# Gate and up projections beside no attention: each 512-token matmul as two of 256 tokens

## The chip, the cores and the metric

The kernel runs on one core of a Trainium2 chip. The metric is the device time of one execution in microseconds (us); smaller is better. "Before" is the kernel as it stands, "after" is the kernel with the change below.

## What is computed

One transformer block on one sequence of 2048 tokens of width 576: a pre-normalised attention with 32 heads of width 18 that share one key and one value head, then a pre-normalised gated feed-forward layer with no nonlinearity.

```
h  = x + softmax(q k^T / sqrt(18)) v @ wo        q, k, v from layernorm(x)
g  = layernorm(h) @ w_gate                       576 -> 4608
u  = layernorm(h) @ w_up                         576 -> 4608
h2 = h + (g * u) @ w_down                        4608 -> 576
```

Every matrix product of the projections is made in a high and a low part: an operand is split into `hi` (rounded to the matmul's number format, fp32r) and `lo` (the rest), and three products hi·hi, hi·lo and lo·hi are summed. That is where the number three in the loops below comes from.

## The kernel before

The tokens are worked on in four blocks of 512 (`TB`), numbered `b` = 0 to 3. A first part makes keys, values, queries and the split weights of the down projection. Then the attention of block `b` + 1 runs beside the feed-forward layer of block `b`: while block 0, 1 and the first part of 2 are in the feed-forward layer (`ffn`), there are still attention pieces to be done, and they are woven in between its matmuls. Attention ends inside block 2. From there to the end the feed-forward layer runs alone: 13 of the 36 steps of block 2 and all 36 of block 3, 49 steps in all. The variable `on` is true while attention is left (`self.more(b + 2)`), and false in those 49 steps.

One step `f` of `ffn` makes 128 of the 4608 gate and up columns for the 512 tokens. The 576 input features lie in nine chunks of 64 (`c`), and each chunk has three products (`wk`, `xk`), 27 in all, counted by `j`. Each of the 27 is a pair of matmuls: gate with the weights in partitions 0 to 63 (`o` = 0) and up with the weights in partitions 64 to 127 (`o` = 64). Both have 64 rows, 128 columns of weights and 512 columns of moving data `X`. Weights are `ws`, already split by `split_w` one step ahead; the moving data is the normalised, transposed input of the block. While `on`, the results go to two PSUM tiles `pg` and `pu`; otherwise to the two halves of one tile `gu`, one bank each:

```
for o, ps in ((0, pg), (64, pu)):
    pe.matmul(ps, w[o:o + 64, wk, c], X[o:o + 64, xk, c], start=(j == 0), stop=(j == 26))
```

Every matmul instruction comes with a weight load of its own in TensorE's instruction stream (the row PEld of the profile), which the engine may run beside an earlier matmul. `start` clears the accumulation marks of the bank that it writes.

After the 27 pairs, ScalarE copies gate out of PSUM (`g`, line 853), VectorE multiplies it with up (`hf`, line 857), and every second step the products are split and combined (`left_first`, `left`, `left_sums`) into the stationary operands `A` of the down projection. `down` (lines 739 to 805) takes two steps' worth of columns at a time, as 14 groups of three matmuls with 288 columns into the tile `y` (line 795, 42 matmuls); its results are added to `h` by VectorE (line 798) or by way of a ScalarE copy (line 802) and GpSimd (line 803). In the stage without attention, TensorE's order is therefore: 54 pairs of two steps, then 42 down matmuls of the steps before, and so on. Nothing schedules this but the order of the program, so each engine runs its instructions in the order in which the code issues them, waiting on semaphores.

`split_w` of the next step is issued at `j == 3`, its weights come by DMA into `wr`; `load_wd` fetches the seven pieces of down weights after each `down`.

Of the kernel before, what the change touches and what calls it, by code (L numbers as in the profile page):

```python
# [27 lines left out]
TB = 512  # L28
# [6 lines left out]
HT = TB // 2  # L35
# [23 lines left out]
class Block:  # L59
# [755 lines left out]
    def ffn(self, b):  # L815
        pe, act, dve = self.pe, self.act, self.dve
        X, hid, todo = self.X, [], None
        for f in range(NF):
            n_ = NF * b + f
            k = f % 2  # L820
            w = self.ws.pop(n_)
            on = self.more(b + 2)
            last = f == NF - 1 and b + 1 < NB
            if on:
                pg, pu = self.ps_f(f"pg{n_}"), self.ps_f(f"pu{n_}")
            else:
                gu = self.ps_s(f"gu{n_}")
                pg, pu = gu[:, 0], gu[:, 1]
            j = 0
            for c in range(9):  # L830
                for wk, xk in ((0, 0), (0, 1), (1, 0)):
                    if on and not last and j % 4 == 0 and self.more(b + 2):
                        self.pair()
                    for o, ps in ((0, pg), (64, pu)):
                        pe.matmul(ps, w[o:o + 64, wk, c], X[o:o + 64, xk, c], start=(j == 0), stop=(j == 26))  # L835
                    if j == (8 if on else 2) and todo and not plain(n_ - 2):
                        self.left_sums()
                    if j == 3:
                        self.split_w(n_ + 1)
                    if j == 5 and k:  # L840
                        self.left_first(n_ - 1, hid[0])
                    if j == 12:
                        self.run_aux(within=True)
                    if j == 21 and b == f == 0:
                        self.flush(len(self.pend))
                    if j == 6 and last:
                        self.normal(b + 1)
                    j += 1
            if todo and not on:
                drain(self.down(b, *todo))  # L850
                self.load_wd(self.n_wd + 7)
            g = self.hh.tile([P, TB], F32, tag="g", bufs=1, name=f"g{n_}")
            act.copy(g, pg)  # L853
            if on and not last and self.more(b + 2):
                self.pair()
            hf = self.hh.tile([P, TB], F32, tag="hf", bufs=2, name=f"hf{n_}")
            dve.tensor_tensor(hf, pu, g, ALU.mult)  # L857
            hid.append(hf)
            if k:
                self.left(n_ - 1, hid)  # L860
                hid = []
            self.flush(len(self.pend))
            if todo and on:
                drain(self.down(b, *todo))
                self.load_wd(self.n_wd + 7)
            if f < NF - 1:
                self.run_aux()
            todo = (f // 2,) if k else None
        if b + 1 < NB:
            both(self.spread(b + 1), self.down(b, *todo))  # L870
            self.load_wd(self.n_wd + 4)
            if b + 2 < NB:
                self.load_x(b + 2)
        else:
            drain(self.down(b, *todo))
# [207 lines left out]
def both(a, b):  # L1083

    live = [a, b]
    while live:
        live = [x for x in live if next(x, drain) is not drain]


def plain(n):  # L1090

    return n % NF == NF - 2
# [23 lines left out]
def drain(gen):  # L1116
    for _ in gen:
        pass
# [78 lines left out]
```

## Time and profile before

| | before |
|---|---|
| time, median of 3 runs | 2339.83 us (2338.97 to 2340.36) |
| the profiled execution's own time | 2337.37 us |
| its span, first to last instruction | 2335.6 us |
| TensorE busy (PE) | 2287.6 us, 98% of the span |
| weight loads busy (PEld) | 1601.8 us, 69% |
| VectorE, ScalarE, GpSimd busy | 50%, 61%, 28% |
| mean granted TensorE clock | 0.995 |
| stage without attention | 1858.4 us to the end |

All rows come from one profiled execution. "PE" rows are matmuls, "PEld" rows are the weight loads, which overlap them. The duration of one matmul in a row is from its start to its end, and the next matmul starts long before that end, so the time that one matmul costs is read from the distance between starts: a row of the timeline that merges n matmuls lasts (n - 1) distances and the duration of one. Line numbers are those of the kernel before; in the kernel after, everything behind line 835 stands two lines further down.

### The profile page before, as it was taken

Reading aid. Unit: us, or ns where it says so; the run is one execution under the profiler, and the core shown is the slowest. Engines: PE = TensorE matmul, PEld = TensorE weight load, DVE = VectorE, ACT = ScalarE, POOL = GpSimd, SP = SyncE. Lnnn points to the kernel's source line nnn. Section 1 sums busy time; section 2 is a strip of 40 time slices with the busy share of each in tenths; the row PEclk is TensorE's granted clock in tenths of the full one; section 3 lists DMA queues with packets and bytes.
Section 4 is the critical chain, followed back from the end, with each engine's and each line's share of the span. In section 5 each row is a group of like instructions: output and inputs, shape, how many; then the busy total and the mean of one; then the engine's idle time right before and its main releaser. Section 6 shows DMA issues by size and latency. Waiting matters only on the chain.

```text
span 2335.6 us, 46068 instructions
## 1 busy us (share of the span) xinstructions
PE 2287.6 (98%) x18225; PEld 1601.8 (69%) x18225; DVE 1175.2 (50%) x2064; ACT 1433.0 (61%) x1867; POOL 650.1 (28%) x803
## 2 busy tenths in 40 slices
PE   5999999999999999999999999999999999999999
PEld 4434434676777777767777766767777778888888
DVE  7566644344444445444444445444444476565665
ACT  4788886767676766667676766667676623222322
POOL 3544500122222221222222221312222234333333
PEclk9999999999999999999999999999999999999999
DMA  4588962343334333533433433634333345655453
GB/s 141 192 275 267 311 204 78 94 128 123 118 123 128 123 121 98 183 116 122 127 121 120 123 119 101 186 119 128 123 123 110 115 141 189 197 188 179 168 168 127
DMA packets 157842, 345.16 MB, mean 148 GB/s; under 512 B 16095, under 2 KB 48351, under 8 KB 157623
## 3 DMA queue, kind: packets, MB, share of 16 engines
q1 hardware_dynamic: 155031, 331.56, 44.4%
q0 software_dynamic: 2592, 10.62, 1.5%
q8 instruction: 145, 2.38, 0.4%
q14 instruction: 74, 0.61, 0.1%
HBM read 272.63 MB, written 55.67 MB: 141 GB/s over the span
## 4 chain that ended last, share of the span: by engine, by line
PE 81%; DVE 2%; issue 1%; ACT 1%; DMA 1%; POOL 0%; SPq 0%; DVEq 0%; ACTq 0%; POOLq 0%
PE y L795 17%; PE pg L835 15%; PE acc L511 15%; PE gu L835 12%; PE pu L835 10%; PE s L506 9%; PE yo L634 3%; PE y L753 1%; ACT P L507 1%; PE ye L753 0%; PE tx L683 0%; DMA X<-X 0%; DMA out_dram<-h 0%; DVE h L798 0%; DVE h L635 0%
## 5 line engine op out<-in xcount | busy, mean ns | idle before, releaser
L507 ACT ACTIVATE P<-s 128x1024 f32<-128x1024 f32 x1024 | 1026.3, 1027 | 305.0 <-PE s L506 226.1
L835 PE MATMUL pg<-X,ws 64*128 64x512 f32 x2565 | 699.8, 391 | 0.0
L835 PE MATMUL pu<-X,ws 64*128 64x512 f32 x2565 | 699.8, 391 | 0.0
L803 POOL TENSOR_TENSOR h<-h,tmp 128x288 f32<-128x288 f32 x408 | 318.6, 810 | 878.7 <-ACT tmp L802 877.2
L835 PEld LDWEIGHTS pg<-X,ws 64*128 64x128 f32 x2565 | 477.0, 186 | 59.7 <-DMA wdo<-wd_dram 0.8
L835 PEld LDWEIGHTS pu<-X,ws 64*128 64x128 f32 x2565 | 474.5, 186 | 35.1
L511 PE MATMUL acc<-P,V 128*32 128x512 f32 x4096 | 490.7, 599 | 0.7 <-ACT P L507 0.6
L506 PE MATMUL s<-q,kT 56*128 56x512 f32 x2048 | 437.1, 423 | 5.0 <-ACT P L507 2.3
L795 PEld LDWEIGHTS y<-wdo,room 128*128 128x128 f32 x2856 | 387.7, 189 | 51.9 <-issue 43.3
L795 PE MATMUL y<-wdo,room 128*128 128x288 f32 x2856 | 404.8, 300 | 4.8 <-DVE h L798 4.8
L802 ACT COPY tmp<-y 128x288 f32<-128x288 f32 x408 | 163.0, 400 | 330.4 <-PE y L795 324.8
L798 DVE TENSOR_TENSOR h<-h,y 128x288 f32<-128x288 f32 x544 | 235.7, 453 | 242.8 <-PE y L795 240.1
L506 PEld LDWEIGHTS s<-q,kT 56*128 56x128 f32 x2048 | 194.0, 184 | 208.4 <-ACT P L507 116.3
L835 PE MATMUL gu<-X,ws 64*128 64x512 f32 x2646 | 308.3, 389 | 0.3 <-DMA X<-X 0.2
L93 POOL CAST ws<-wr 128x1152 fp32r<-128x1152 f32 x144 | 168.2, 1168 | 430.9 <-PE pu L835 172.6
L835 PEld LDWEIGHTS gu<-X,ws 64*128 64x128 f32 x2646 | 250.8, 184 | 51.3 <-issue 4.0
L511 PEld LDWEIGHTS acc<-P,V 128*32 128x32 f32 x4096 | 114.4, 109 | 247.7 <-issue 241.9
L94 DVE TENSOR_TENSOR ws<-wr,ws 128x1152 fp32r<-128x1152 f32 x144 | 195.6, 1358 | 79.7 <-POOL ws L93 79.7
L857 DVE TENSOR_TENSOR hf<-pu,g 128x512 f32<-128x512 f32 x95 | 65.7, 692 | 332.2 <-ACT g L853 332.2
L94 DVE TENSOR_TENSOR room<-S,room 128x1024 fp32r<-128x1024 f32 x68 | 83.3, 1225 | 159.0 <-ACT room L93 159.0
L853 ACT COPY g<-gu 128x512 f32<-128x512 f32 x49 | 28.9, 590 | 134.8 <-PE gu L835 134.8
L93 ACT CAST room<-hf 128x256 fp32r<-128x256 f32 (+1 forms) x144 | 73.9, 513 | 49.2 <-DVE hf L857 49.0
(162 smaller groups left out, 1572.0 us busy)
## 6 DMA issues: line engine op xcount, KB each, us to landing
wdo<-wd_dram SPq DMA_DIRECT2D x492, 288.0 KB
wr<-in_wgu_dram SPq DMA_DIRECT2D x144, 576.0 KB
wd_dram<-wd_room SPq DMA_DIRECT2D x20, 1008.0 KB
q<-q_dram SPq DMA_DIRECT2D x64, 216.0 KB
q_dram<-qs SPq DMA_DIRECT2D x16, 504.0 KB
X<-X SPq DMA_DIRECT2D x28, 256.0 KB
wd_dram<-wd_hi SPq DMA_DIRECT2D x7, 1008.0 KB
wd_dram<-wd_src SPq DMA_DIRECT2D x7, 1008.0 KB
```

The source lines that it names most:

```text
L93: (copy or self.cast)(hi, src)
L94: self.dve.tensor_tensor(lo, src, f32(hi), ALU.subtract)
L506: self.pe.matmul(s_[:, i], self.kT[o:o + 56, t * P:(t + 1) * P], q[o:o + 56, pr], start=True, stop=True)
L507: self.act.activation(p_, s_, AF.Exp, scale=SCALE)
L511: self.pe.matmul(acc[32 * j:32 * j + 32, :], self.V[:, t, :], Ps[j // 2][:, j % 2, :], start=(t == 0), stop=(t == NT - 1), skip_group_chec ...
L634: pe.matmul(y[:, :HD], m, k, start=(i == 0), stop=(i == len(ms) - 1))
L795: pe.matmul(y[:, :HD], m[:, t * P:(t + 1) * P], k, start=(first and j == 0), stop=(j == 2), skip_group_check=True)
L798: dve.tensor_tensor(hs, hs, y[:, :HD], ALU.add)
L802: act.copy(z, y[:, :HD])
L803: pool.tensor_tensor(hs, hs, z, ALU.add)
L835: pe.matmul(ps, w[o:o + 64, wk, c], X[o:o + 64, xk, c], start=(j == 0), stop=(j == 26))
L857: dve.tensor_tensor(hf, pu, g, ALU.mult)
```

## The change

In the 49 steps without attention, each pair of 512-column matmuls becomes two pairs of 256 columns: first gate and up for the first 256 tokens, then gate and up for the other 256, with the same weights. While attention is beside them, the loop body is what it was.

```diff
-                    for o, ps in ((0, pg), (64, pu)):
-                        pe.matmul(ps, w[o:o + 64, wk, c], X[o:o + 64, xk, c], start=(j == 0), stop=(j == 26))
+                    for t in range(0, TB, TB if on else HT):
+                        q = slice(t, t + (TB if on else HT))
+                        for o, ps in ((0, pg), (64, pu)):
+                            pe.matmul(ps[:, q], w[o:o + 64, wk, c], X[o:o + 64, xk, c, q], start=(j == t == 0), stop=(j == 26), skip_group_check=not on)
```

`HT` is 256. The mark-clearing `start` stays on the very first matmul of each bank; the second half's first matmul finds the marks of its columns cleared and overwrites. In the instruction order of the kernel after, 54 gate and up matmuls of a step without attention have become 108 of 256 columns; ScalarE, VectorE, GpSimd and the DMA queues have the same instructions and the same waits, in the same order.

## The prediction
> **What bounds the kernel now.** I read the page first: its busy line and its chain. Then the stage that the change touches, by windows, and then single stretches of TensorE's timeline, because the price of a matmul is the distance between two starts.
>
> ```profile
> span 2335.6 us, 46068 instructions
> PE 2287.6 (98%) x18225; PEld 1601.8 (69%) x18225; DVE 1175.2 (50%) x2064; ACT 1433.0 (61%) x1867; POOL 650.1 (28%) x803
> ...
> PE 81%; DVE 2%; issue 1%; ACT 1%; DMA 1%; POOL 0%; SPq 0%; DVEq 0%; ACTq 0%; POOLq 0%
> ```
>
> TensorE is busy for 98% of the span and makes 81% of the chain that ended last. Whatever lengthens its stream lengthens the kernel. The stage without attention, whole and then line 835 alone:
>
> ```profile
> 1858.30:2324.50 466.20, 459.40 (x3723) 397.20 (x3721) 285.00 (x505) 135.78 (x267) 168.96 (x198) 1.00 0.52 172
> ```
> ```profile
> 1858.30:2324.50 466.20, 308.21 (x2646) 250.79 (x2646) 1.00 0.52 172
> ```
>
> The columns are PE, PEld, DVE, ACT and POOL busy, the granted clock, DMA share and GB/s. TensorE works 459.40 of 466.20 us; VectorE has 181 us free, the others more, and DMA is half used. So nothing covers a longer TensorE, and nothing else becomes late before it does. Gate and up have 308.21 us there: 49 steps of 27 pairs, 1323 pairs. Loads are busy 250.79 us in it.
>
> **The price of a pair now.**
>
> ```profile
> 1891.71 6.51 PE L835 MATMUL gu<-X,ws 64*128 64x512 f32 x56
> ```
> ```profile
> L835 PEld LDWEIGHTS gu<-X,ws x2646: 182/184/187, 1858.4 to 2323.9; 64*128 64x128 f32 x189
> L835 PE MATMUL gu<-X,ws x2646: 383/386/501, 1858.4 to 2324.2; 64*128 64x512 f32 x189
> ```
>
> 56 matmuls are 28 pairs: (6.51 - 0.386) / 27 = 226.8 ns from pair to pair, so 113.4 ns is what half a pair may cost for the change to be free. The maximum of 501 ns against a median of 386 is a matmul that had to wait for its own load, at the head of a stretch: one load uncovered costs some 115 ns. That it is 115 and not twice this says that the two loads of a pair (rows 0 to 63 and 64 to 127) run side by side. And since the ordinary matmul takes 386, its load is covered.
>
> **The change part by part.** It adds, per pair, two matmuls and two loads; 2646 of each in all. It moves nothing else: the other engines' order and waits stay, every `j` still comes at the same place, and the last matmul of a step, on which ScalarE's copy waits, is still the last. The columns streamed per pair are the same 512. So the question is what 256 columns cost with a load each time. Three things can set it: the stream, the load, the start.
>
> The load. The row that shows loads alone is the one in which the matmul has nearly no columns:
>
> ```profile
> 55.95 1.44 PE L312 MATMUL psv<-C,kvw 18*128 18x18 f32 x12 [2.66 <-DVE kvw L239]
> ```
> ```profile
> L312 PE MATMUL psv<-C,kvw x16: 261/268/288, 55.9 to 58.5; 18*128 18x18 f32 x16
> ```
>
> (1.44 - 0.268) / 11 = 106.5 ns from one 128-column load to the next, with 18 columns of matmul. This is the floor of half a pair, however fast the stream: 2 x 106.5 = 213.0, 13.8 ns below today's pair, times 1323 is 18 us less. The loads of the stretch of 56 matmuls above, which began at 1891.71, begin here:
>
> ```profile
> 1891.72 0.41 PEld L835 LDWEIGHTS gu<-X,ws 64*128 64x128 f32 x4
> ```
>
> So the next pair's loads start within 0.01 us of this pair's matmuls. 106.5 fits under 113.4, with 7 ns to spare less that start. Today the spare is 120 ns. I take the load as covered, but barely.
>
> The start. The short matmuls of this stage are the down projection's, 288 columns with a load of 128 columns each:
>
> ```profile
> 2149.82 3.54 PE L795 MATMUL y<-wdo,room 128*128 128x288 f32 x25
> ```
> ```profile
> L795 PEld LDWEIGHTS y<-wdo,room x2856: 186/188/330, 436.9 to 2317.8; 128*128 128x128 f32 x191
> L795 PE MATMUL y<-wdo,room x2856: 288/295/442, 436.9 to 2317.9; 128*128 128x288 f32 x191
> L795 PEldq EVENT_SEMAPHORE  x410: 51/51/51, 441.2 to 2316.7; - x137
> ```
>
> (3.54 - 0.295) / 24 = 135.2 ns per matmul. At the rate of the long pair (226.8 / 512 = 0.443 ns per column) 288 columns would be 127.6, so a short matmul costs 7.6 ns more than its columns. Not all of this need come back here: these matmuls have 410 extra semaphore waits on the load side among them, and all 128 rows in one load. The ends for a half are then 113.4 (nothing per start) and 121.0 (all 7.6). I take the middle, 117.2, because the row's 7.6 ns holds waits that gate and up don't have, and because I see no row of short matmuls that costs nothing extra. Per pair 2 x 117.2 - 226.8 = 7.6 ns; times 1323 = **10.1 us**. The ends are 0 and 2 x 7.6 x 1323 = 20.1 us.
>
> The head of each stretch stays. Two steps together show it:
>
> ```profile
> 2153.28 12.54 PE L835 MATMUL gu<-X,ws 64*128 64x512 f32 x108
> ```
>
> 53 x 226.8 + 386 = 12406 ns, so 0.13 us of 12.54 are the head, one uncovered load of the same 128 columns and a few uneven pairs. The load before the first matmul is as long after the change; cost nothing, as nothing about it changes.
>
> Who waits on the longer stretch: ScalarE for the copy out of `gu`, GpSimd for `ws` to come free, VectorE for `g`.
>
> ```profile
> ACT g L853 <- PE gu L835: 134.8, 26, 8.4
> ...
> POOL ws L93 <- PE gu L835: 102.1, 22, 8.0
> DVE hf L857 <- ACT g L853: 84.2, 25, 4.6
> ```
>
> All of them wait for TensorE already, none the other way; they wait longer by what TensorE loses, and nothing else comes late. TensorE itself waits for hardly anything in this stage but this:
>
> ```profile
> PE y L795 <- DVE h L798: 4.8, 2, 3.6
> ```
>
> 3.6 us of it is one stall, for VectorE's additions, and does not hang on line 835's length.
>
> The sum against the profiled execution: 2337.37 + 10.1 = 2347.5 us. Its median neighbours are 2.46 us higher (2339.83), so **2349.9 us** in a median of runs, 0.43% slower.
>
> **A rule against the trace.** The Trainium skill, "TensorE: Matmul & The Clock Gate", Part 3 on packing small matmuls, says that a weight load overlaps a matmul in flight only when it targets another row group. This trace does not agree: the load for rows 0 to 63 has only matmuls of its own row group and of the other half before it, and the 386 against 501 ns show it covered. By the rule each half would show its load, 113.4 + 106.5, a pair 440 ns, and the kernel 282 us longer; the long pairs of today would show it too, so I give it no chance of its own.
>
> **The rivals.**
>
> *Nothing happens.* Load 106.5 under stream 113.4, no cost per start: 2340 us, up to 2344 with a ns or so per matmul. For it: 7 ns of margin, and no wait in the chain that belongs to loads. Against it: the 7.6 ns of the 288-column row. It would also come out so if the second load of the same weights were left out; that it isn't is shown by line 795, where two of each three matmuls have the same stationary operand and there are still 2856 loads for 2856 matmuls. Chance 0.24.
>
> *Faster.* The long pair's 226.8 ns may hold something per matmul that grows with its length, such as a stall late in the stream when the load is long done, and shorter matmuls would shed it. Then the load's pace sets the half. Between the floor of 106.5 and 113.4 it would be about 110, a pair 220, 6.8 ns x 1323 = 9 us less: 2331 us. It decides as soon as half a pair is under 111.6 ns (4.7 us less). Nothing in the rows shows it. Chance 0.07.
>
> *The supply of instructions.* A pair is now four instructions in 226.8 ns, 57 each. The densest long stretch I find is the attention's value matmuls:
>
> ```profile
> 1849.41 3.18 PE L511 MATMUL acc<-P,V 128*32 128x512 f32 x27
> ```
> ```profile
> L511 PE MATMUL acc<-P,V x4096: 592/592/1061, 64.9 to 1852.0; 128*32 128x512 f32 x196
> ```
>
> Groups of four, six distances in 3.18 - 0.592: 431 ns for eight instructions, 54 each. The change asks for eight in 226.8, 28 each, twice what any stretch shows. If the queue can't be fed faster than these rows, a pair takes 431 ns and the kernel (431 - 227) x 1323 = 270 us more, 2610 us. Against it: the value matmuls are themselves bound by their columns (512 each, none of the 3.18 us idle), so 54 is what they ask for and not a limit that they show. The same size of loss would come if two loads of different rows took turns (213 per half, 199 ns per pair, 263 us), which the 501 ns of the head speaks against. Together 0.09.
>
> The same page, Part 2 on issuing a matmul, gives some 62 ns per matmul in the sequencer where the hardware does not decode them: an estimate of 4 x 62 = 248 ns per pair, 28 us more. The rows above have no long stretch with matmuls closer than 106 ns on average, so none can refuse it.
>
> *A middle loss.* Half a pair between 121 and 127 ns, because load and start add up where the spare is 7 ns (106.5 + 7.6 + the few ns by which the load starts late): up to 2 x 13.6 x 1323 = 36 us, 2360 to 2376. Chance 0.14.
>
> **How the numbers follow.** My forecast case, a half between 115.2 and 121 ns, 2344.5 to 2360 us, has 0.46. A measurement of this kernel can tell about 0.2%, 4.7 us, from no change. Faster 0.07; same 0.24; slower 0.46 + 0.14 + 0.09 = 0.69. The range runs from 2337 (the no-change case with its noise) to 2372 (most of the middle loss); outside lie the faster case, the supply case and a little of the middle loss, about 0.2.
>
> **What the profile after would show.** Line 837 with 5292 matmuls and 5292 loads on `gu`, 64x256. Two steps together, 216 matmuls, last 12.54 us now; at my price 12.54 + 54 x 0.0076 = 12.95, less what a shorter last matmul saves. A merged row of n matmuls gives the half pair directly: 113 says that loads and starts are hidden, 117 my forecast, 121 the full start cost, 125 and more that load and start add up, 215 that supply or loads in turn bind. The 42 down matmuls between should keep their 5.9 us. I am wrong if the half pair is outside 115 to 121, or if the time moves in another line than 837.

## The result and the profile after

The kernel after takes 2349.37 us (median of 5 runs, 2348.63 to 2354.76), the kernel before 2338.97 in the same comparison (2337.3 to 2340.36): 1.005 times as long, 95% interval 1.0036 to 1.0065. The forecast was 2349.9. The total is right; the steps behind it are right less often, as the traces show, and part of the agreement is luck.

The page after, its first lines and its chain:

```profile
span 2347.1 us, 51360 instructions
PE 2300.3 (98%) x20871; PEld 1665.0 (71%) x20871; DVE 1169.8 (50%) x2064; ACT 1431.8 (61%) x1867; POOL 645.9 (28%) x803
...
PE 82%; DVE 1%; ACT 1%; issue 1%; POOL 0%; DMA 0%; SPq 0%; DVEq 0%; ACTq 0%; POOLq 0%
```

5292 instructions more, 2646 matmuls and 2646 loads, and TensorE as full as before. The stage without attention now, line 837 alone (PE and PEld busy, with their counts):

```profile
1857.20:2336.00 478.80, 324.10 (x5292) 318.98 (x5292) 1.00 0.51 168
```

Before, loads were busy 250.79 of 308.21 us; now 318.98 of 324.10. That alone doesn't say that loads set the pace. The pace is read from a merged stretch (a row that merges n matmuls of one line), the durations of single matmuls and loads from the group of line 837:

```profile
1891.83 3.40 PE L837 MATMUL gu<-X,ws 64*128 64x256 f32 x54
...
2158.47 13.21 PE L837 MATMUL gu<-X,ws 64*128 64x256 f32 x216
2171.61 5.92 PE L795 MATMUL y<-wdo,room 128*128 128x288 f32 x42
```
```profile
L837 PEld LDWEIGHTS gu<-X,ws x5292: 182/188/190, 1857.2 to 2335.6; 64*128 64x128 f32 x196
L837 PE MATMUL gu<-X,ws x5292: 271/280/385, 1857.2 to 2335.8; 64*128 64x256 f32 x196
```

54 matmuls are 27 half pairs: (3.40 - 0.280) / 26 = 120.0 ns from half to half, where 113.4 was the price of no change. Two steps together last 13.21 us instead of 12.54, and the 42 down matmuls behind them 5.92, as before. So the loss is in line 837.

Where the span's 11.5 us are, summed over the distances between neighbouring matmul starts in both traces:

| between starts of | before, us | after, us | difference |
|---|---|---|---|
| gate and up to gate and up (2621 and 5267 distances) | 298.97 | 317.24 | +18.3 |
| last gate and up matmul to first down matmul (23) | 7.25 | 4.72 | -2.5 |
| the same, to the transposes and to the last block's end (2) | 0.63 | 0.41 | -0.2 |
| within the down matmuls (990) | 143.81 | 140.94 | -2.9 |
| first matmul of the kernel to the first of the stage | 1844.15 | 1842.82 | -1.3 |

The rest of the span, 40.8 us before and 40.9 after, is the other matmuls of the stage and the two ends.

The second row is a real saving of the change: the down matmuls start 205 ns after the start of the last gate and up matmul instead of 315, since that one is 280 ns long instead of 386. 1.2 us of the fourth row come from the change, too: TensorE's two waits for VectorE (`PE y L795 <- DVE h L798`) are 3.6 us together instead of 4.8, the longer one 2.9 instead of 3.6 (total, number, longest; after):

```profile
PE y L795 <- DVE h L798: 3.6, 2, 2.9
```

In the longer one, VectorE is held up by weights of the output projection (`wor`), which SyncE fetches during the stretch of gate and up ahead of these down matmuls and GpSimd casts. The timeline before and then after, transfer, first down matmul and cast:

```profile
1870.51 0.47 SPq L596 DMA_DIRECT2D wor<-in_wo_dram  x1
...
1870.85 1.45 PE L795 MATMUL y<-wdo,room 128*128 128x288 f32 x9
...
1873.40 0.67 POOL L93 CAST wos<-wor 128x576 fp32r<-128x576 f32 x1 [7.38 <-DMA wor<-in_wo_dram]
```
```profile
1869.17 0.47 SPq L596 DMA_DIRECT2D wor<-in_wo_dram  x1
...
1870.34 1.46 PE L795 MATMUL y<-wdo,room 128*128 128x288 f32 x9
...
1872.21 0.67 POOL L93 CAST wos<-wor 128x576 fp32r<-128x576 f32 x1 [7.05 <-DMA wor<-in_wo_dram]
```

The transfer starts 0.34 us ahead of the down matmuls before, 1.17 us after: the longer stretch covers more of it. The runs below bear this out. The two waits together fall as the two steps get longer: 4.8 us at 12.54 (before), 4.3 at 12.82 (narrower weights), 3.6 at 13.21 (after), 3.1 at 13.51 (unequal parts), 0.9 at 14.53 (parts of 288 columns).

The rest of the fourth row, and the fifth, are not the change's. In the profiled execution of before, the clock that TensorE was granted fell to half for 3.4 us twice, here behind the longer wait; in that of after it did not at these places. The same part of the down matmuls (window, matmuls and loads, clock), before and then after:

```profile
1876.70:1880.10 3.40, 3.40 (x16) 3.40 (x15) 0.50 0.32 87
```
```profile
1875.40:1878.80 3.40, 3.39 (x26) 3.16 (x24) 1.00 0.45 104
```

A down matmul takes 240 ns at the clock of 0.50, against a median of 132 at 1.00, and the 15 distances from the first slowed matmul on are 1.5 us longer than the same 15 after. The other such stretch, 1378.3 to 1381.7 us, lies ahead of the stage, in instructions that both kernels share, and costs 1.5 us as well. It isn't the split that spares after this: the run below with the split in all steps has such a stretch behind the same wait (1893.5 to 1896.9). So 3.0 us of the 4.2 in these two rows are an accident of the two executions that were profiled.

### The profile page after: what moved, and what is told of

It is laid out like the page before. It is cut to its first block, busy times and chain, and to the rows that moved or that the text cites. A ratio compares the mean times of both kernels' runs of the same rounds, so it can differ in the third digit from the quotient of the medians.

```text
span 2347.1 us, 51360 instructions
## 1 busy us (share of the span) xinstructions
PE 2300.3 (98%) x20871; PEld 1665.0 (71%) x20871; DVE 1169.8 (50%) x2064; ACT 1431.8 (61%) x1867; POOL 645.9 (28%) x803
## 4 chain that ended last, share of the span: by engine, by line
PE 82%; DVE 1%; ACT 1%; issue 1%; POOL 0%; DMA 0%; SPq 0%; DVEq 0%; ACTq 0%; POOLq 0%
PE y L795 17%; PE pg L837 15%; PE acc L511 15%; PE gu L837 13%; PE pu L837 10%; PE s L506 9%; PE yo L634 3%; PE y L753 1%; ACT P L507 1%; PE tx L683 0%; PE ye L753 0%; SPq L568 0%; POOL h L803 0%; DVE h L798 0%; DMA wdo<-wd_dram 0%
## 5 line engine op out<-in xcount | busy, mean ns | idle before, releaser
L795 PEld LDWEIGHTS y<-wdo,room 128*128 128x128 f32 x2856 | 385.9, 188 | 45.6 <-issue 35.2
L795 PE MATMUL y<-wdo,room 128*128 128x288 f32 x2856 | 402.9, 300 | 3.6 <-DVE h L798 3.6
L798 DVE TENSOR_TENSOR h<-h,y 128x288 f32<-128x288 f32 x544 | 234.9, 453 | 249.9 <-PE y L795 249.9
L837 PE MATMUL gu<-X,ws 64*128 64x256 f32 x5292 | 324.1, 281 | 0.0
L837 PEld LDWEIGHTS gu<-X,ws 64*128 64x128 f32 x5292 | 319.0, 188 | 4.1 <-issue 4.1
```

Of the source, the lines that this page charges most:

```text
L795: pe.matmul(y[:, :HD], m[:, t * P:(t + 1) * P], k, start=(first and j == 0), stop=(j == 2), skip_group_check=True)
L798: dve.tensor_tensor(hs, hs, y[:, :HD], ALU.add)
L837: pe.matmul(ps[:, q], w[o:o + 64, wk, c], X[o:o + 64, xk, c, q], start=(j == t == 0), stop=(j == 26), skip_group_check=not on)
```

## The experiments

The question is why half a pair takes 120.0 ns. Three things could set it: a cost that each matmul has for itself (theory A), the load (B), or the supply of instructions (C). All edits are to the four lines of the kernel after, and only the lines that differ are shown; what the steps with attention do stays, unless said. Quarters, the halves with 64 columns of weights and the whole scan were measured in one execution each, the other runs in 4 or 10.

**Unequal parts.**

```diff
-for t in range(0, TB, TB if on else HT):
-    q = slice(t, t + (TB if on else HT))
+for t, n in ((0, TB),) if on else ((0, 288), (288, 224)):
+    q = slice(t, t + n)
```

> The two parts are 288 and 224 columns instead of 256 and 256: as many matmuls, loads and columns. After showed 120.0 ns per half pair, where the long pair takes 226.7 per 512 columns. Theory A, every matmul has a start cost of its own: the two sizes give 0.4167 ns per column and 13.3 ns per matmul, so 133.3 + 106.7 = 240 ns per pair, as in after: same time as after, 2349 us. Theory B, the load sets the pace: from a load's start to the next load's start 120 ns pass (106.5 for the load, 13.5 to take it over), and the columns cost only what they cost in the long pair. Then the 224 part can't be under 120 and the 288 part takes 127.5 to 133.3: 247.5 to 253.3 per pair, 10 to 18 us more than after, 2359 to 2367 us. Theory C, instructions come no faster than four per 120 ns: as B.

Measured: 2355.75 us, 1.0077 times before (1.0061 to 1.0094). Two steps together:

```profile
2201.83 13.51 PE L837 MATMUL gu<-X,ws 64*128 64x288 f32 x216
```

0.30 us more than after in 54 pairs, 5.5 ns per pair: 245.5, between A's 240 and the lower end of B and C. The 224-column part is followed by the next start after a median of 102 ns, which no theory of a 120 ns floor allows. What is left over A's 240 is taken up again behind the quarters.

**Quarters.**

```diff
-for t in range(0, TB, TB if on else HT):
-    q = slice(t, t + (TB if on else HT))
+for t in range(0, TB, TB if on else P):
+    q = slice(t, t + (TB if on else P))
```

> Four parts of 128 columns instead of two of 256, so four loads per row group and pair. Theory A: the columns and the start cost are 53.3 + 13.3 = 66.7 ns, less than a load, so the load's pace as the transposed values show it, 106.5 ns, up to 110 with the late start, sets each part: 426 to 440 ns per pair, about 250 us more than after at 106.5 and 265 at 110, 2595 to 2615 us. Theory B and theory C: each part 120 ns, 480 per pair, 318 us more than after, 2665 us.

Measured: 2614.79 us, and

```profile
2258.43 24.34 PE L837 MATMUL gu<-X,ws 64*128 64x128 f32 x432
```
```profile
L837 PE MATMUL gu<-X,ws x10584: 268/272/326, 1854.9 to 2601.7; 64*128 64x128 f32 x200
```

(24.34 - 0.272) / 215 = 111.9 ns per part. B and C, with 120, are out: loads repeat faster than the half pairs of after do, and so do instructions, four in 112 ns, 28 ns each. The floor is 112 here and not the 106.5 of the transposed values. With that the sum of the unequal parts comes out: 133.3 for the 288 columns by A, and the 224 held up at 111.9 instead of 106.7, together 245.2 ns. The parts one by one do not: the medians are 141 ns behind a 288-column part and 102 behind a 224-column one. So that the floor holds up the short part there is an inference from the sum.

**Narrower weights.** If each matmul has a cost of its own, the width of its weights doesn't matter.

```diff
+m = P if on or j in (0, 26) else 96
-pe.matmul(ps[:, q], w[o:o + 64, wk, c], X[o:o + 64, xk, c, q], ...
+pe.matmul(ps[0:m, q], w[o:o + 64, wk, c, 0:m], X[o:o + 64, xk, c, q], ...
```

> As after, but the weights of 25 of the 27 pairs of a step have 96 columns instead of 128, so three quarters of a load; the fourth quarter of the gate and up columns is left out of the sum in the stage without attention. Theory A (a start cost per matmul): half a pair stays at 120, 2349 us. Theory B (the load's pace): a load takes 80 and its takeover 13.5, 93 ns, less than the columns, so the half falls to 113.4, the long pair's rate, and the kernel to 2337 to 2340 us. Theory C (supply of instructions): stays at 120, 2349 us.

Measured: 2343.48 us, 1.0024 times before (1.0013 to 1.0035). The halves take 116.2 ns in the mean, neither 120 nor 113.4, and unevenly: the distances are 113, 117 or 121 ns by turns. Two steps together:

```profile
2101.37 12.82 PE L837 MATMUL gu<-X,ws 64*128 64x256 f32 x216
```

A, which wants 120, is not right as it stands either, and B's 113.4 isn't met. So I formed a theory D: a matmul pays for the reading of the load that runs beside it, 13.3 ns for 128 columns of weights. It gives 116.7 here. It was tried on whole pairs and on halves.

```diff
-for t in range(0, TB, TB if on else HT):
+for t in range(0, TB, TB):                     # the two whole-pair runs; the half run keeps HT
+m = P if on or j in (0, 26) else 96            # then 64, 64
```

The matmul takes the first `m` columns of weights, as in the run before.

> The pairs are whole again (512 columns, as before the change), but the weights of 25 of the 27 pairs of a step have 96 columns; the fourth quarter of gate and up is left out of the sum there. Theory A, a start cost of 13.3 ns per matmul, whatever its load: 226.7 ns per pair as before, 2338 us. Theory D, what a matmul pays is the reading of the load beside it, 13.3 ns for 128 columns and in proportion for fewer (the narrow half pairs took 116 instead of 120): 213.3 + 10.0 = 223.3 ns per pair, 3.3 x 1225 pairs = 4 us less than before, 2334 us.

> As the one with 96 columns, but 64 columns of weights in 25 of the 27 pairs; half of gate and up is left out there. Theory A: 226.7 ns per pair. Theory D: 213.3 + 6.7 = 220.0 ns per pair, 8 us less than before. The first and the last pair of a step keep 128 columns and so another tile shape, which may cost a drain of some 100 ns twice a step, up to 10 us in either theory; so the pace within the 25 decides, not the time.

> Halves of 256 columns as in after, with 64 columns of weights in 25 of the 27 pairs. Theory A: 120 ns per half. Theory D: 106.7 + 6.7 = 113.3 ns per half, so a pair as long as before the change.

Measured: with 96 columns 2339.61 us, 1.001 times before (1.0 to 1.002), with 64 columns 2340.99, 1.0017 times (1.0008 to 1.0027), and the halves with 64 columns 2334.58. Two steps together in their three timelines, in that order:

```profile
2099.96 12.71 PE L837 MATMUL gu<-X,ws 64*128 64x512 f32 x108
```
```profile
2117.29 12.70 PE L837 MATMUL gu<-X,ws 64*128 64x512 f32 x108
```
```profile
2113.55 12.57 PE L837 MATMUL gu<-X,ws 64*128 64x256 f32 x216
```

The whole pairs got longer with less to load (12.71 and 12.70 us against 12.54; 230.0 ns per pair in the mean, where D wants 223.3 and 220.0). The halves with 64 columns did what D said, 113.65 ns. One theory can't have both: D falls on the whole pairs, A on the halves, and A's 226.7 misses the whole pairs as well. These runs also write fewer rows of the result, so the load is not all that differs in them. That left the load itself, slowed by the stream beside it (theory E), and called for a scan.

**A scan of the columns.** Two parts per pair, 128 columns of weights, other widths of a part; then halves with two more widths of weights, `m` = 112 and `m` = 32, as above.

```diff
-for t in range(0, TB, TB if on else HT):
-    q = slice(t, t + (TB if on else HT))
+for t, n in ((0, TB),) if on else ((0, HT), (HT, HT)) if j in (0, 26) else ((0, 192), (HT, 192)):
+    q = slice(t, t + n)            # then ((0, 224), (HT, 224)) and ((0, 288), (224, 288))
```

> A scan of the columns of a part, two parts per pair in 25 of the 27 pairs, weights of 128 columns; here 192 columns each, so 128 of the 512 tokens are left out of those products. Left standing: Theory D, a matmul costs N x 0.4167 ns and 13.3 ns for the reading of a 128-column load beside it, and a load can't be repeated under the 112 ns that the quarters showed: 93.3 is under it, so 112 ns per part. Theory E, a matmul costs in proportion to its columns, 0.443 ns each as in the long pair (113.4 for 256, as the narrowest weights showed), and what takes 120 in after is the load: 106.7 ns alone, 112 with a matmul of 128 columns beside it and 120 with one of 256, because the stream beside it slows its reading: about 116 ns per part.

> As the scan's first, with parts of 224 columns; 64 of 512 tokens are left out of those products. Theory D: 93.3 + 13.3 = 106.7, under the load's 112, so 112 ns per part. Theory E: the load, slowed by the stream, about 118 ns per part.

> As the scan's first, with parts of 288 columns that overlap by 64, so 64 tokens get those products twice. Theory D: 120 + 13.3 = 133.3 ns per part. Theory E: the columns bind again, 288 x 0.443 = 127.5 ns, up to 131 where the pairs run unevenly; the load's 120 is hidden.

> Halves of 256 columns with weights of 112 columns in 25 of the 27 pairs; an eighth of gate and up is left out there. Theory D: 106.7 + 11.7 = 118.3 ns per half. Theory E: the load takes 112/128 of 117, 102 ns, and 3 ns of start, under the columns' 113.4, so 113.4 ns, up to 116.5 where the pairs run unevenly as with 96 columns.

> Halves of 256 columns with weights of only 32 columns in 25 of the 27 pairs; three quarters of gate and up are left out there. So far parts of 128, 192 and 224 columns took 111 to 112 ns, 256 took 120 with 128 columns of weights, 116.2 with 112 and with 96, 113.7 with 64, and 288 took 132. Theory D, 13.3 ns of load reading per 128 columns of weights: 106.7 + 3.3 = 110 ns per half. Theory P, the columns alone cost 0.443 ns each, 113.4 for 256, and the load adds to that only where its own pace of 112 comes near: 113.4, no lower than with 64 columns.

Times: 2334.36, 2330.73, 2372.96, 2341.63 and 2344.82 us. Two steps together, in the timelines of the parts of 192, 224 and 288 columns, then of the halves with 112 and with 32 columns of weights (a merged row names the form of its first matmul; in the first three, 16 of the 216 are the 256-column ones of the first and last pair of each step):

```profile
2097.41 12.38 PE L837 MATMUL gu<-X,ws 64*128 64x256 f32 x216
```
```profile
2238.89 12.38 PE L837 MATMUL gu<-X,ws 64*128 64x256 f32 x216
```
```profile
2170.98 14.53 PE L837 MATMUL gu<-X,ws 64*128 64x256 f32 x216
```
```profile
2229.17 13.00 PE L837 MATMUL gu<-X,ws 64*128 64x256 f32 x216
```
```profile
2082.71 12.99 PE L837 MATMUL gu<-X,ws 64*128 64x256 f32 x216
```

Mean distance from part to part, within the pairs of the width in question and without the few distances of over 300 ns:

| moving columns | weight columns | ns per part | N x 0.4167 + 13.3 | N x 0.443 |
|---|---|---|---|---|
| 128 | 128 | 111.9 | 66.7 | 56.7 |
| 192 | 128 | 111.3 | 93.3 | 85.1 |
| 224 | 128 | 111.6 | 106.7 | 99.2 |
| 256 | 128 | 120.0 | 120.0 | 113.4 |
| 288 | 128 | 131.9 | 133.3 | 127.6 |
| 512 | 128 | 226.8 | 226.7 | 226.8 |
| 256 | 112 | 116.2 | 120.0 | 113.4 |
| 256 | 96 | 116.2 | 120.0 | 113.4 |
| 256 | 64 | 113.7 | 120.0 | 113.4 |
| 256 | 32 | 116.3 | 120.0 | 113.4 |
| 512 | 96, 64 | 230.0 | 226.7 | 226.8 |

The row of 512 and 128 is from the stretch of 56 matmuls; by this mean it is 227.3. The line N x 0.4167 + 13.3 is drawn through the rows of 256 and 512 with 128 columns of weights.

Two things are settled by it. First, up to 224 columns the part costs the same 111 to 112 ns: that is a floor which the columns beside it do not raise, against theory E. At 256 columns a part is 8 ns above it, so in the kernel after the load is hidden. I read the floor as the load's pace. The runs don't show that: each of the three has four instructions per part as well, so a supply of one instruction in 28 ns would give the same 112, and only short parts with narrow weights would tell the two apart. Second, with 128 columns of weights the columns' price from 256 to 512 is a straight line with 13.3 ns per matmul, 1.4 ns off at 288. In the two half-clock stretches of before these 13 ns are not there: 288 columns in 240 ns and 512 in some 425 are both 0.83 ns per column. The remaining rows are not settled: with other widths of weights 256 columns cost 113.7 to 116.3, with no order in the width (32 columns are no better than 112), and 512 cost 230. With 112 columns the halves came out as E said (113.4 to 116.5), not as D did (118.3); with 32 neither D's 110 nor theory P's 113.4 was met. The distances within such runs jump between a few values. What picks among 113, 116 and 120 ns for the same 256 columns stays open; all of them lie above the floor, and the size of the load gives no order.

**The split beside attention as well.**

```diff
-for t in range(0, TB, TB if on else HT):
-    q = slice(t, t + (TB if on else HT))
+for t in range(0, TB, HT):
+    q = slice(t, t + HT)
```

> The split also in the steps with attention beside them, 2565 more pairs. There a pair takes 231 to 237 ns now, 233 in the mean. Theories A and B: halves of 120, 240 per pair, 7 ns x 2565 = 18 us more than after, 2367 us, if TensorE is as much the bound there as the chain says. If ScalarE's exponentials hide part of it, less than that.

Measured: 2368.23 us, 1.0132 times before (1.0115 to 1.0149), 18.9 us above after, which was measured in another comparison. The gate and up line with attention beside it (windows, matmuls and loads), before and then with the split everywhere:

```profile
399.00:1858.00 1459.00, 705.13 (x5130) 497.85 (x5130) 1.00 0.40 124
```
```profile
399.00:1875.00 1476.00, 725.10 (x10262) 713.25 (x10262) 1.00 0.39 123
```

The 20.0 us that it is busier are in the time almost whole. Halves follow each other there after 119.8 ns in the mean, so the price of a half is the same in both stages, and ScalarE's exponentials hide none of it. No version tried here that computes the whole result beats the kernel before.

## Why the prediction was right

**What bounds.** Right in the main. TensorE's stream sets the stage, and nothing else became late; the other engines' rows moved by less than 1%. One sentence was wrong: that the 3.6 us stall for VectorE does not hang on the length of the line. It fell to 2.9, and the second wait by 0.5, so 1.2 us of the longer stream were covered by waits.

**The load, covered but barely.** Right, with a wrong size: I took its pace as 106.5 ns from the transposed values, and the floor with two row groups is 111 to 112. I also overlooked the clock of that row: it lies in a stretch of half clock (window, busy times, clock),

```profile
55.90:57.40 1.50, 1.44 (x12) 1.35 (x12) 0.63 (x1) 0.00 (x0) 0.77 (x1) 0.50 0.03 8
```

while the stage without attention has 1.00. Whether the clock or the second row group makes the difference, no run here shows. The cover of 256 columns is 8 ns because a half takes 120, and it would be 2 ns at 113.4. With 224 columns it is gone.

**The start, 117.2 ns per half.** This is the term that was mis-sized: 120.0. I halved the 7.6 ns by which the down matmuls exceed their columns, as containing waits; 6.6 of it came back, near the upper end of 121. Over 2646 halves the 2.8 ns are 7.4 us: 17.5 us in place of 10.1, and the table has 18.3 with the uneven pairs and the heads. That short matmuls of this shape pay something that columns alone do not explain held for weights of 128 columns. That it is a start, paid once by every matmul, is not shown: the same number of matmuls with narrower weights costs 113.7 to 116.3. Why they pay it is open.

**The last matmul of a stretch.** I named its saving and gave it no number. It is 0.11 us at 25 places, 2.7 us. It works against the loss, and it is one reason why a term too small by 7 us gave a total right within 1.

**The sum.** 18.3 - 2.7 in line 837's own stretches, then -2.9 in the down matmuls and -1.3 ahead of the stage, neither foreseen: 11.4 us in the two profiled executions, 10.4 between the medians. Of these 4.2 us, 1.2 are the shorter waits and 3.0 the stretches of half clock that only before had. Without them the change costs 18.3 - 2.7 - 1.2 = 14.4 us, an estimate from these two traces. The runs on record agree: three of the five of after have a mean clock of 0.996 and take 2348.6 to 2349.4 us, and the nine of before with 0.996, in the comparisons of the experiments, have a median of 2334.8. It also lies within the measured interval, which is 8.4 to 15.2 us. So, as far as these figures go, the total was met within 1 us by luck: the clock hid what the term of the start was too small by.

**The rivals.** "Nothing happens" needed 113.4 and "faster" less: 120.0. For "faster" the floor of 111.6 would have made the gain 5 us. "The supply of instructions", as it was priced, is out: the quarters take four instructions in 112 ns over stretches of 24 us. So is its second form, loads of the two row groups by turns: two loads in 112 ns are not two in 213. "A middle loss", load and start added up, is out as well: it wanted 121 to 127, and at 224 columns a load and whatever its start adds take 111.6.

**The two rules.** The Trainium skill, "TensorE: Matmul & The Clock Gate", Part 2 on issuing a matmul, gives some 62 ns per matmul where the hardware does not decode it, an estimated 248 ns for a pair. The quarters have a matmul every 56 ns, so this does not bind on this chip as it is run. The Trainium skill, "TensorE: Matmul & The Clock Gate", Part 3 on packing small matmuls, says that a load overlaps matmuls in flight only when it is for another row group. The runs contradict it more plainly than the trace before: with it, a quarter could not be shorter than its load and its columns together, and parts of 128 and of 224 columns take the same time, 111.9 and 111.6 ns.

## What to carry to other kernels

Price a matmul that carries its own load as the larger of two: the floor at which load and matmul repeat, and the columns with a sum on top; take both from rows of the same tile shape and the same granted clock, not from one that merely looks like it. Splitting the stream that the engine is bound by cost such a sum here even though every load is hidden: 6.6 ns per half with weights of 128 columns, and 0.5% of the kernel. Before a small difference between two profiles is put down to a change, compare the granted clock along both: two stretches of 3.4 us at half clock were worth 3.0 us here. A load row that is 98% busy is no proof that loads bind: ask whether the pace changes when only the columns do.

## What the runs showed of the hardware that was not expected

A matmul with a load of 128 columns repeats after 111 to 112 ns with two row groups side by side, with 128, 192 and 224 columns alike. TensorE took an instruction every 28 ns over the quarters' stretches of 24 us. And fewer weight columns made the 512-column pairs slower, 230.0 ns against 226.8, while they made the 256-column halves faster, 113.7 to 116.3 against 120.0. And the granted clock fell to 0.50 for 3.4 us in the middle of a busy kernel (before, 1876.7 us, just behind a wait of 3.6 us; the unequal parts, 1874.1, behind one of 2.5): a 288-column matmul then takes 240 ns. After has a wait of 2.9 us and no such stretch, so the length of the wait alone does not decide it.
